# Tuned attention + gMLP kernel: PSUM banks handed out by longest free, products in single banks, and scores placed directly behind a product

## The chip, the cores and the metric

The kernel runs on one core of one Trainium2 chip. The metric is device time in microseconds, median of three runs. All engines of the core take part: TensorE (PE, with its weight loads PEld), VectorE (DVE), ScalarE (ACT), GpSimd (POOL), and SyncE (SP), which issues the transfers.

## The reference

Batch is 8, heads 8, sequence 576, head dimension 64; d_model is 512 and d_ff 1024.

```python
scores = scale * q @ k.T                      # per batch and head
scores = where(block_i >= block_j, scores, -1e9)   # blocks of 64
attn = exp(scores - max); attn = attn / (sum(attn) + 1e-9)
x = (attn @ v) laid out as (B, S, 512)
h = relu(x @ w_in); u, v = h[..., :512], h[..., 512:]
v_n = (v - mean) / sqrt(var + 1e-6)
v_s = einsum('ts,bsd->btd', w_spatial, v_n) + b_spatial
out = (u * v_s) @ w_out
```

## The kernel before

Work is cut by batch, and in a batch by pairs of heads: four pairs per batch, 32 pairs, named b_p (7_3 is the last) and numbered g = 4b + p. Batch 0 has its own opening; batch 1 ("plain") uses the raw q and k; from batch 2 on q and k are split in a high and a low part (`hi`, `lo`).

A pair goes through these steps. SP loads `raw`; ACT, DVE and POOL make `hi` and `lo`. TensorE makes the scores in four parts (lane "S"): parts 0 and 1 in a PSUM tile of two banks each (a double), part 2 in two single banks, part 3 (`scores_last`, called L below, line L568) in a double again. DVE's `rows` (L614, L620) read the scores out of PSUM with the mask and the row maximum; ACT takes exp; POOL and ACT scale; DVE transposes in blocks of 32 (L683); sixteen transfers on SP's queue (L691) regroup the blocks from `p` to `pt`, of which there is one buffer. Then TensorE makes the product (lane "A", tile `av`, L709): a low part of 4 matmuls for the first 256 rows and a high part of 18 for the other 320. Both lie in one double. ACT copies each half out and DVE subtracts (L746), which gives `x`.

The gMLP of a batch (lane "M") is 360 matmuls: `mv` (v half, L1062), `mu` (u half, L1172), `ms` (spatial product, L1209 to L1216), `mo` (output, L1261). Each group of them fills one single bank, which ACT or DVE empties. The first v group of a batch needs all four products of that batch.

PSUM's eight banks are two doubles (`ps_s`, ring `r_s`) and four singles (`ps_m`, ring `r_m`). A ring hands its buffers out in turn: the next taker gets the buffer that was given out longest ago, whether another one is free or not.

Nothing is in the order in which the functions add it. All steps are given to `Line`, which plays them against costs written in the kernel (ns per step, `TURN` for a change of kind on TensorE, `REACH` for a signal) and so fixes each engine's instruction order; on the chip every engine follows its order and waits on semaphores. On TensorE `pick_pe` takes the head of a lane: S and A wait until their inputs have been ready for `SLACK` ns, and the first part of a pair's scores has a gate: not before the M matmuls done (`spent`) amount to (g - LEAD)/4 of a batch's gMLP. In what follows one unit is such a quarter. Where the plan leaves TensorE idle for long, `bridge` fills the gap with pad matmuls (as many as fit in the gap less 300 ns, and none for fewer than three).

Of the kernel before, what the change touches and what calls it, by code (L numbers as in the profile page):

```python
# [17 lines left out]
P = 128  # L18
# [17 lines left out]
LEAD = 5.0  # L36
# [3 lines left out]
    ("A", "S"): 200, ("A", "M"): 250, ("A", "T"): 203, ("M", "A"): 96, ("T", "A"): 96,  # L40
}
REACH = {"PE": 170, "DVE": 125, "ACT": 145, "POOL": 70}
SLACK = {"A": 3500, "S": 1200, "T": 0, "M": 100}


class Ring:
# [5 lines left out]
    def free_at(self, ahead=0):  # L52
        k = len(self.given) + ahead - self.bufs
        if k < 0:
            return 0.0
        if k >= len(self.given) or self.given[k].users:
            return None
        return self.given[k].freed

# [17 lines left out]
class Line:  # L77
# [48 lines left out]
    def pick_pe(self):  # L126
# [12 lines left out]
        late = [k for k in at if not (k == "S" and heads[k].gate is not None and self.spent < heads[k].gate and "M" in at)]  # L139
# [5 lines left out]
    def bridge(self, until):  # L145
# [8 lines left out]
        self.spare.given.append(hold)  # L154
        self.pad("M" if self.kind == "T" else self.kind, n)

    def pick(self, eng):
        if eng == "PE":
            return self.pick_pe()
# [27 lines left out]
    def play(self):  # L187
        while True:
            picks = [(p[0], e, p[1]) for e in self.ENGINES for p in [self.pick(e)] if p]
            if not picks:  # L190
                break
# [3 lines left out]
            for h in op.takes:  # L195
                h.ring.given.append(h)
# [5 lines left out]
            if eng == "PE":  # L202
# [3 lines left out]
                self.kind, self.run = kind, op.first and op.lane  # L206
# [23 lines left out]
def kernel(  # L230
# [32 lines left out]
    ps_s = ctx.enter_context(tc.tile_pool(name="ps_s", bufs=2, space=PSUM))  # L263
    ps_m = ctx.enter_context(tc.tile_pool(name="ps_m", bufs=4, space=PSUM))
# [11 lines left out]
    warm = ps_m.tile([P, 512], F32, tag="m", name="warm")  # L276
# [24 lines left out]
    r_m, r_s = Ring(4), Ring(2)  # L301
# [3 lines left out]
    def pad(kind, n):  # L305
        x = ps_m.tile([P, 512], F32, tag="m", name=f"pad_{next(pads)}")
# [12 lines left out]
    def given(ring, users):  # L319
        h = Hold(ring, users)  # L320
        ring.given.append(h)
        return h

    given(r_m, 0)
# [138 lines left out]
    u_tile = {}  # L463
# [4 lines left out]
    def banks(k, nm):  # L468

        if k == 2:  # L470
            return [ps_m.tile([P, 512], F32, tag="m", name=f"s_{nm}_2_{hd}") for hd in range(2)]
        x = ps_s.tile([P, 2, 512], F32, tag="s", name=f"s_{nm}_{k}")
# [7 lines left out]
    def attention(b, pr):  # L480
# [61 lines left out]
        def scores(k):  # L542
            bk = box["s", k] = banks(k, nm)
# [14 lines left out]
        def scores_last():  # L558
            bk = ps_s.tile([P, 2, 512], F32, tag="s", name=f"s_{nm}_3")
# [15 lines left out]
        for k in range(4):  # L575
# [123 lines left out]
        def start_product():  # L699
            box["av"] = ps_s.tile([P, 2, 512], F32, tag="s", name=f"av_{nm}")  # L700

# [3 lines left out]
        def products(z, todo):  # L705
            for n, (c, q0, q1, move) in enumerate(todo):
                for j in range(2):
                    js = slice(64 * j, 64 * j + 64)
                    nc.tensor.matmul(  # L709
                        box["av"][js, z, q0:q1], box["v"][:, c, js], move(j), start=(n == 0),  # L710
# [3 lines left out]
        def low_product():  # L714
            start_product()
# [14 lines left out]

        a_hold = Hold(r_s, 4)
        al = line.add("PE", 646, low_product, after=[*moved, got_v], takes=[a_hold], lane="A")
        al.first = True
        al.slack = 500 if plain else None
        ah = line.add("PE", 2082, high_product, behind=[al], lane="A", drops=[pt_hold, v_hold])
        ev = []
        for z, (q0, n, src) in enumerate(((0, 256, al), (256, 320, ah))):
            def high(z=z, q0=q0, n=n):
# [4 lines left out]
                nc.scalar.copy(box["x"][:, 0, q0:q0 + n], box["av"][:, z, :n])  # L743

            def low(z=z, q0=q0, n=n):
                nc.vector.tensor_tensor(  # L746
                    out=box["x"][:, 1, q0:q0 + n], in0=box["av"][:, z, :n],
# [6 lines left out]
            h = add("ACT", (269, 321)[z], high, after=[src], takes=takes, drops=[a_hold], rank=0,  # L754
                    behind=ev[:1])
            ev.append(add("DVE", (335, 402)[z], low, after=[h], drops=[a_hold], rank=0))
# [10 lines left out]
    def opening():  # L767
# [65 lines left out]
        def unit(k, pr):  # L833
# [8 lines left out]
            def scores():  # L842
# [7 lines left out]
                if k == 3:  # L850
                    box["s"] = bk = ps_s.tile([P, 2, 512], F32, tag="s", name=f"s_{nm}")
# [5 lines left out]
                box["s"] = bk = banks(k, nm)  # L857
# [77 lines left out]
            for z, (t0, m) in enumerate(split):  # L935
                t_hold = Hold(r_m, 1)

                def transposes(z=z, t0=t0, m=m):
                    box["t", z] = ps_m.tile([P, 512], F32, tag="m", name=f"t_{nm}_{z}")
# [24 lines left out]
            def product():  # L964
                box["av"] = ps_s.tile([P, 2, 512], F32, tag="s", name=f"av_{nm}")
# [63 lines left out]
    def moe(b, ready):  # L1029
# [14 lines left out]
        def v_group(c):  # L1044
# [5 lines left out]
            def bank():  # L1050
                if "ps" not in box:
                    box["ps"] = ps_m.tile([P, 512], F32, tag="m", name=f"mv_{b}_{c}")
                return box["ps"]

# [5 lines left out]
            def mm(n, j, k, w):  # L1060
                a = tails[b][:, k].rearrange("p j t -> p (j t)") if j == 2 else xts[b, k][:, j, cs]
                nc.tensor.matmul(bank(), a, w[:, k, DH:], start=(n == 0), stop=(n == len(todo) - 1))  # L1062
# [99 lines left out]
        def u_group(z, dc):  # L1162
# [6 lines left out]
            def mm(n, j, k, w):  # L1169
                if n == 0:  # L1170
                    box["ps"] = ps_m.tile([P, 512], F32, tag="m", name=f"mu_{b}_{z}_{dc}")
# [25 lines left out]
        def sp_group(z, dc):  # L1197
# [8 lines left out]
            def mm(n, k, a, w):  # L1206
                if n == 0:
                    box["ps"] = ps_m.tile([P, 512], F32, tag="m", name=f"ms_{b}_{z}_{dc}")
# [165 lines left out]
```

## Time and profile before

| | us |
|---|---|
| median of 3 runs | 691.52 (691.37 to 692.26) |
| the profiled execution | 691.11 |
| its span, first to last instruction | 689.3 |
| TensorE busy in it | 664.6 (96%) |
| DVE busy | 495.6 (72%) |
| ACT busy | 369.5 (54%) |
| POOL busy | 344.9 (50%) |

The span is the time between the first and the last instruction; 1.8 us of the execution lie around it. Ends of matmuls are modelled and overlap, so below the distance from one start to the next is used for what a matmul costs.

### The profile page before, as it was taken

Reading aid. Unit: us, or ns where it says so; the run is one execution under the profiler, and the core shown is the slowest. Engines: PE = TensorE matmul, PEld = TensorE weight load, DVE = VectorE, ACT = ScalarE, POOL = GpSimd, SP = SyncE. Lnnn points to the kernel's source line nnn. Section 1 sums busy time; section 2 is a strip of 40 time slices with the busy share of each in tenths; the row PEclk is TensorE's granted clock in tenths of the full one; section 3 lists DMA queues with packets and bytes.
Section 4 is the critical chain, followed back from the end, with each engine's and each line's share of the span. In section 5 each row is a group of like instructions: output and inputs, shape, how many; then the busy total and the mean of one; then the engine's idle time right before and its main releaser. Section 6 shows DMA issues by size and latency. Waiting matters only on the chain.

```text
span 689.3 us, 15505 instructions
## 1 busy us (share of the span) xinstructions
PE 664.6 (96%) x5394; PEld 582.2 (84%) x5394; DVE 495.6 (72%) x1404; ACT 369.5 (54%) x1036; POOL 344.9 (50%) x689
## 2 busy tenths in 40 slices
PE   8999889999999999999999999999999999999998
PEld 5586767888889888988889888898889888898897
DVE  6989789767885778767787678857787677842532
ACT  7879757644654565455655546544654546511320
POOL 4377644545665445664555456644456645520111
PEclk9999999999999999999999999999999999999999
DMA  8164566566456664566555654566645555441002
GB/s 282 48 214 145 143 175 189 152 167 164 126 140 169 159 167 115 130 164 169 142 135 136 162 149 128 135 169 154 159 124 139 152 159 152 98 110 56 1 1 70
DMA packets 44210, 95.57 MB, mean 139 GB/s; under 512 B 9698, under 2 KB 19938, under 8 KB 44132
## 3 DMA queue, kind: packets, MB, share of 16 engines
q1 hardware_dynamic: 44132, 94.58, 50.9%
q8 instruction: 43, 0.70, 0.5%
q14 instruction: 35, 0.29, 0.1%
HBM read 39.23 MB, written 9.44 MB: 71 GB/s over the span
## 4 chain that ended last, share of the span: by engine, by line
PE 32%; DMA 17%; SPq 15%; DVE 14%; ACT 11%; POOL 6%; issue 5%; DVEq 0%; ACTq 0%; POOLq 0%
SPq L691 15%; DMA raw<-qk 11%; PE ms L1209 7%; PE mo L1261 7%; DMA pt<-p 5%; DVE p L683 4%; PE av L709 4%; POOL p L337 4%; DVE p L614 4%; PE mv L1062 3%; ACT hi L516 3%; PE mu L1172 3%; ACT p L642 2%; DVE x L746 2%; PE t L949 2%
## 5 line engine op out<-in xcount | busy, mean ns | idle before, releaser
L642 ACT ACTIVATE p<-p,nmax 128x128 f32<-128x128 f32 (+4 forms) x252 | 145.9, 581 | 50.3 <-DVE nmax L614 39.6
L337 POOL TENSOR_SCALAR p<-p,ssum 128x384 f32<-128x384 f32 (+5 forms) x262 | 151.9, 593 | 20.9 <-DVE ssum L661 6.7
L683 DVE STREAM_TRANSPOSE p<-p 128x384 f32<-128x384 f32 (+2 forms) x196 | 122.2, 641 | 28.5 <-POOL p L337 26.7
L1172 PE MATMUL mu<-x,wi_hi 128*128 128x288 f32 x512 | 110.3, 299 | 1.8 <-ACT vr L1074 1.8
L614 DVE CUSTOM_DVE_ANT_1 p<-s,mask 128x128 f32<-128x128 f32 (+1 forms) x224 | 95.0, 486 | 3.1 <-PE s L552 2.4
L655 POOL TENSOR_SCALAR ssum<-ssum 128x4 f32<-128x4 f32 (+1 forms) x112 | 26.6, 237 | 125.9 <-ACT p L642 111.4
L709 PE MATMUL av<-pt,v 128*64 128x64 f32 (+2 forms) x1232 | 83.0, 290 | 6.4 <-DMA pt<-p 4.8
L709 PEld LDWEIGHTS av<-pt,v 128*64 128x64 f32 x1232 | 65.3, 137 | 27.7 <-issue 10.4
L1172 PEld LDWEIGHTS mu<-x,wi_hi 128*128 128x128 f32 x512 | 85.3, 190 | 3.5 <-ACT vr L1074 2.0
L1062 PE MATMUL mv<-wi_hi,x 128*128 128x512 f32 x256 | 87.4, 400 | 0.0
L1261 PE MATMUL mo<-gh,wo_hi 128*128 128x288 f32 x256 | 76.5, 299 | 0.2
L1209 PE MATMUL ms<-ws_lo,vh 128*128 128x288 f32 x256 | 76.6, 299 | 0.0
L1209 PE MATMUL ms<-ws_hi,vh 128*128 128x288 f32 x256 | 76.5, 299 | 0.0
L1261 PE MATMUL mo<-gh,wo_lo 128*128 128x288 f32 x256 | 76.1, 297 | 0.0
L1261 PE MATMUL mo<-gl,wo_hi 128*128 128x288 f32 x256 | 76.0, 297 | 0.0
L1209 PE MATMUL ms<-ws_hi,vl 128*128 128x288 f32 x256 | 75.7, 296 | 0.0
L1172 PE MATMUL mu<-x,wi_lo 128*128 128x288 f32 x256 | 70.8, 298 | 1.2 <-POOL wi_lo L361 1.2
L516 ACT CAST hi<-raw 128x640 fp32r<-128x640 f32 x48 | 33.3, 726 | 60.2 <-DMA raw<-qk 56.8
L522 POOL TENSOR_TENSOR lo<-raw,hi 128x320 fp32r<-128x320 f32 (+1 forms) x72 | 53.8, 763 | 19.9 <-ACT hi L516 19.9
L1231 ACT CAST gh<-u 128x288 fp32r<-128x288 f32 x64 | 26.4, 429 | 62.7 <-DVE u L1223 45.0
L1062 PEld LDWEIGHTS mv<-wi_hi,x 128*128 128x128 f32 x256 | 48.1, 188 | 12.4 <-issue 2.9
L1234 POOL TENSOR_TENSOR gl<-u,gh 128x288 fp32r<-128x288 f32 x48 | 38.2, 810 | 28.9 <-ACT gh L1231 28.4
(130 smaller groups left out, 1502.9 us busy)
## 6 DMA issues: line engine op xcount, KB each, us to landing
pt<-p SPq DMA_DIRECT2D x448, 100.0 KB, 2.2
raw<-qk SPq DMA_DIRECT2D x28, 640.0 KB, 4.5
v<-v SPq DMA_DIRECT2D x32, 320.0 KB, 3.1
outT<-o SPq DMA_DIRECT2D x64, 144.0 KB, 2.0
rwi<-w_in SPq DMA_DIRECT2D x8, 512.0 KB, 4.3
rwo<-w_out SPq DMA_DIRECT2D x4, 512.0 KB, 4.0
raw<-qk SPq DMA_DIRECT2D x8, 192.0 KB, 4.6
rws<-w_spT SPq DMA_DIRECT2D x4, 288.0 KB, 2.8
```

The source lines that it names most:

```text
L337: nc.gpsimd.tensor_scalar(out=x, in0=x, scalar1=by, scalar2=1.0, op0=ALU.mult, op1=ALU.mult)
L516: nc.scalar.copy(box["hi"][:, cs], box["raw"][:, cs])
L522: eng.tensor_tensor(out=box["lo"][:, cs], in0=box["raw"][:, cs], in1=box["hi"][:, cs].bitcast(F32), op=ALU.subtract,)
L614: nc.vector.tensor_tensor_reduce(out=out, in0=by_block(bk[hd][:, o:o + n]), in1=tiles(mask, 5 - t, t + 1), scale=-0.125, scalar=BIG, op0=A ...
L642: nc.scalar.activation(out, out, AF.Exp, bias=mx, scale=-1.0, accum_out=box["sum", k][:, c:c + 1],)
L683: nc.vector.transpose(x, x)
L691: nc.sync.dma_start(box["pt"][32 * j:32 * j + 32, i], box["pp"][32 * i:32 * i + 32, j])
L709: nc.tensor.matmul(box["av"][js, z, q0:q1], box["v"][:, c, js], move(j), start=(n == 0), stop=(n == len(todo) - 1), skip_group_check=True,)
L1062: nc.tensor.matmul(bank(), a, w[:, k, DH:], start=(n == 0), stop=(n == len(todo) - 1))
L1172: nc.tensor.matmul(box["ps"][:, :HT], w[:, k, ds], xts[b, k][:, j, zs], start=(n == 0), stop=(n == len(todo) - 1),)
L1209: nc.tensor.matmul(box["ps"][:, :HT], vn[k][a][:, ds], w[:, k, zs], start=(n == 0), stop=False)
L1261: nc.tensor.matmul(box[ec, "ps"][:, :HT], w[:, k, es], a[:, k, :], start=(k == 0 and n == 0), stop=(last and n == 2),)
```

## The change

Seven edits, of which the first four belong together.

- Banks are handed out by a new ring, `Banks`: a taker gets the one that has been free longest, and each bank has a tag of its own, so that no taker waits for a certain bank in turn.
- The product's two halves take one single bank each (`a_holds`, in `r_m`) and no double.
- From pair 2_2 on (`MATE + 2`), the first scores of pair g have no gate of their own: they stand directly behind the product of pair g-2 (`first`, `trail`), and that product waits until the `hi` and `lo` of pair g are there. The product has the gate instead, at (g + 2 - 5.5)/4 of a batch for its own g. `op.first` now names the lane that must follow, so parts 0, 1 and 2 of the scores and the product before them stay together; `pick_pe` gets a first try (`hold`) in which such a run is not broken up.
- For the pairs before, `LEAD` is 6 units in place of 5.
- `SLACK` of a product is 2500 in place of 3500 ns (100 in place of 500 in batch 1), and `TURN` from A to S 110 in place of 200.
- In a batch's gMLP seven `ms` groups, not six, stand ahead of the first four `mo` groups; in batch 0 the fifth v group comes one place sooner.
- Making `w_out`'s halves has a lower rank (2.6 in place of 2.1).

```diff
-LEAD = 5.0
+LEAD = 6.0
+MATE, MATE_LEAD = 8, 5.5
...
-SLACK = {"A": 3500, "S": 1200, "T": 0, "M": 100}
+SLACK = {"A": 2500, "S": 1200, "T": 0, "M": 100}
...
+class Banks(Ring):
+    def __init__(self, bufs):
+        self.last = [None] * bufs
+    def free(self):
+        return sorted((h.freed if h else 0.0, n) for n, h in enumerate(self.last) if not h or not h.users)
+    def free_at(self, ahead=0):
+        free = self.free()
+        return free[ahead][0] if ahead < len(free) else None
+    def take(self, hold):
+        hold.at = self.free()[0][1]
+        self.last[hold.at] = hold
...
+        if hold and self.run and self.run == self.kind and self.run in heads and not heads[self.run].left:
+            return None
...
-            if k == "S" and op.gate is not None and self.spent < op.gate and "M" in heads:
+            if k in "SA" and op.gate is not None and self.spent < op.gate and "M" in heads:
...
+    def bank(hold, name):
+        return ps_m.tile([P, 512], F32, tag=f"m{hold.at}", name=name)
+
+    def double(hold, name):
+        return ps_s.tile([P, 2, 512], F32, tag=f"s{hold.at}", name=name)
...
-            op.first = k < 2
+            op.first = "S" if k < 2 else None
             op.waive = k == 3
             if k == 0:
-                op.gate = (g - LEAD) * MOE_NS / NPAIR
+                if g < MATE + 2:
+                    op.gate = (g - LEAD) * MOE_NS / NPAIR
+                else:
+                    first, last = mates[g - 2]
+                    last.trail.append(op)
+                    op.left += 1
+                    for d in need:
+                        d.trail.append(first)
+                    first.left += len(need)
...
-        a_hold = Hold(r_s, 4)
-        al = line.add("PE", 646, low_product, after=[*moved, got_v], takes=[a_hold], lane="A")
-        al.first = True
-        al.slack = 500 if plain else None
-        ah = line.add("PE", 2082, high_product, behind=[al], lane="A", drops=[pt_hold, v_hold])
+        a_holds = [Hold(r_m, 2), Hold(r_m, 2)]
+        al = line.add("PE", 646, low_product, after=[*moved, got_v], takes=a_holds[:1], lane="A")
+        al.first = "A"
+        if g >= MATE:
+            al.gate = (g + 2 - MATE_LEAD) * MOE_NS / NPAIR
+        al.slack = 100 if plain else None
+        ah = line.add("PE", 2082, high_product, behind=[al], takes=a_holds[1:], lane="A", drops=[pt_hold, v_hold])
+        ah.first = "S" if MATE <= g < B * NPAIR - 2 else None
+        mates[g] = al, ah
...
-        order = "vuvuvuvuvuuuu" if b else "vvvvuuuuuuvuu"
+        order = "vuvuvuvuvuuuu" if b else "vvvvuuuuuvuuu"
...
-        return front[:1], front[1:] + sp[:ND + 2] + out[:NO] + sp[ND + 2:], out[NO:]
+        return front[:1], front[1:] + sp[:ND + 3] + out[:NO] + sp[ND + 3:], out[NO:]
...
-    ready["o"] = [x for c in range(ND) for x in prep_w_out(c, 2.1)]
+    ready["o"] = [x for c in range(ND) for x in prep_w_out(c, 2.6)]
```

What the plan makes of it is seen in the order of instructions. First TensorE at the scores of pair 7_3. In the names `s_7_3_0` is part 0 of the scores, `s_7_3_3` the last part L, `mu_6_1_3` an M group of batch 6, `av_7_1` the product of pair 7_1; the last number of a name only tells buffers apart. Before:

```order
L1172 MATMUL mu_6_1_3_8019<-x_6_2_7137,wi_hi_114 128x288
L1172 MATMUL mu_6_1_3_8019<-x_6_3_7409,wi_hi_114 128x288
L552 MATMUL s_7_3_0_8039<-hi_7_3_7904 128x128 x2
L552 MATMUL s_7_3_0_8039<-lo_7_3_7905,hi_7_3_7904 128x128 x2
L552 MATMUL s_7_3_0_8039<-hi_7_3_7904,lo_7_3_7905 128x128 x2
```

and now:

```order
L750 MATMUL av_7_1_1_8010<-pt_7_1_7762,v_7_1_7660 64x64 x2
L750 MATMUL av_7_1_1_8010<-pt_7_1_7762,v_7_1_7660 64x128 x2
L750 MATMUL av_7_1_1_8010<-pt_7_1_7762,v_7_1_7660 64x64 x4
L587 MATMUL s_7_3_0_8038<-hi_7_3_7876 128x128 x2
L587 MATMUL s_7_3_0_8038<-lo_7_3_7877,hi_7_3_7876 128x128 x2
L587 MATMUL s_7_3_0_8038<-hi_7_3_7876,lo_7_3_7877 128x128 x2
```

The scores moved from behind an M group to behind a product; this is so at 22 pairs (2_2 to 7_3), and at pair 1_3. Between the first three parts and L stand 9 M matmuls for pair 7_3 now, and 12 before.

Next DVE ahead of the rows of the same pair. `vr`, `st`, `vl` and `vs_a` belong to the normalization of v groups 3 and 4 of batch 6, `x_7_1` is the product's subtraction. Before:

```order
L1122 TENSOR_SCALAR vr_6_3_7872<-vr_6_3_7872,st_6_3_7873 128x512
L1187 TENSOR_SCALAR u_6_7632<-mu_6_1_2_7995 128x288
L1154 TENSOR_TENSOR vl_6_3_8013<-vr_6_3_7872,vh_6_3_8012 128x512
L1122 TENSOR_SCALAR vr_6_4_7918<-vr_6_4_7918,st_6_4_7919 64x512
L1187 TENSOR_SCALAR u_6_7632<-mu_6_1_3_8019 128x288
L1138 TENSOR_TENSOR vs_a_122<-vr_6_4_7918,vs_b_123 64x512
L614 ISA p_7_3_8074,nmax_7_3_0_8075<-s_7_3_0_8039,mask_93 128x4x32
```

and now:

```order
L1163 TENSOR_SCALAR vr_6_3_7940<-vr_6_3_7940,st_6_3_7941 128x512
L1123 TENSOR_TENSOR vr_6_4_7998<-mv_6_4_7957,vr_6_4_7998 64x512
L1127 TENSOR_SCALAR vr_6_4_7998<-vr_6_4_7998 64x512
L790 TENSOR_TENSOR x_7_1_8032<-av_7_1_0_8003,x_7_1_8032 128x256
L1135 BN_STATS st_6_4_7999<-vr_6_4_7998 64x6
L1136 BN_AGGR st_6_4_7999<-st_6_4_7999 64x2
L1195 TENSOR_TENSOR vl_6_3_8030<-vr_6_3_7940,vh_6_3_8029 128x512
L790 TENSOR_TENSOR x_7_1_8032<-av_7_1_1_8010,x_7_1_8032 128x320
L657 ISA p_7_3_8067,nmax_7_3_0_8068<-s_7_3_0_8038,mask_93 128x4x32
```

The rows moved ahead of the last two steps of v group 4, and behind the product's two subtractions.

Last, the pads on TensorE, of which before there were 3, 8, 8 and 14, and now 3, 17, 13, 3, 11 and 4. The first 3 are in the opening; the 17 stand ahead of the first `mu` group, the 13 ahead of the first `ms` group, the 3 ahead of the product 2_1, the 11 ahead of the product 2_3, the 4 ahead of the last product, 7_3. The row of the last ones before:

```order
L1209 MATMUL ms_6_1_3_8375<-ws_hi_118,vl_6_3_8013 128x288
L1214 MATMUL ms_6_1_3_8375<-ws_a_120,vs_a_122 128x288
L1216 MATMUL ms_6_1_3_8375<-ws_b_121,vs_b_123 128x288
L314 MATMUL pad_3_8396<-ident_92 128x128 x14
L709 MATMUL av_7_3_8411<-pt_7_3_8243,v_7_3_7955 64x256 x2
```

and now:

```order
L1250 MATMUL ms_6_1_3_8424<-ws_hi_118,vl_6_3_8030 128x288
L1255 MATMUL ms_6_1_3_8424<-ws_a_120,vs_a_122 128x288
L1257 MATMUL ms_6_1_3_8424<-ws_b_121,vs_b_123 128x288
L350 MATMUL pad_5_8453<-ident_92 128x128 x4
L750 MATMUL av_7_3_0_8458<-pt_7_3_8300,v_7_3_8204 64x256 x2
```

The place is the same, ten pads fewer. Between the scores L of pair 7_3 and the product 7_2 stand 82 M matmuls now and 45 before; between the products 7_2 and 7_3 stand 102 (103 before). On SP's queue two stores stand between the sixteen transfers of `pt_7_3` now, four before.

More of the change, by code (lines that the diff above doesn't have):

```diff
@@ L153, in bridge, with pick @@
         hold.freed = now + n * PAD_NS
-        self.spare.given.append(hold)
-        self.pad("M" if self.kind == "T" else self.kind, n)
-    def pick(self, eng):
+        self.spare.take(hold)
+        self.pad("M" if self.kind == "T" else self.kind, n, hold)
+    def pick(self, eng, hold):
         if eng == "PE":
-            return self.pick_pe()
+            return self.pick_pe(hold)
         now, best = self.free[eng], None
@@ L188, in play @@
         while True:
[L189 to L190 removed]
+            for hold in (True, False):
+                picks = [(p[0], e, p[1]) for e in self.ENGINES for p in [self.pick(e, hold)] if p]
+                if picks:
+                    break
+            else:
                 break
@@ L205, in play @@
                 end = start + TURN.get((self.kind, kind), 0) + ns
-                self.kind, self.run = kind, op.first and op.lane
+                self.kind, self.run = kind, op.first
                 if kind == "M" and op.lane == "M":
@@ L300, with pad @@
     add = line.add
-    r_m, r_s = Ring(4), Ring(2)
     r_raw, r_hi, r_lo, r_v, r_pp, r_pt, r_x, r_xs = (Ring(n) for n in (1, 1, 1, 2, 2, 1, 6, 2))
     r_u, r_gh, r_gl, r_vr, r_o, r_vn, r_vs = (Ring(n) for n in (1, 1, 1, 2, 2, 1, 1))
-    def pad(kind, n):
-        x = ps_m.tile([P, 512], F32, tag="m", name=f"pad_{next(pads)}")
+    def pad(kind, n, hold):
+        x = bank(hold, f"pad_{next(pads)}")
         for k in range(n):
@@ L459, in prep_w_tail, with banks @@
         return [a, b, c, d, e]
-    u_tile = {}
+    mates = {}
     def by_block(x):
         return x.rearrange("p (j x) -> p j x", j=4)
-    def banks(k, nm):
+    def banks(k, nm, holds):
         if k == 2:
-            return [ps_m.tile([P, 512], F32, tag="m", name=f"s_{nm}_2_{hd}") for hd in range(2)]
-        x = ps_s.tile([P, 2, 512], F32, tag="s", name=f"s_{nm}_{k}")
+            return [bank(holds[hd], f"s_{nm}_2_{hd}") for hd in range(2)]
+        x = double(holds[0], f"s_{nm}_{k}")
         return x[:, 0], x[:, 1]
@@ L558, in scores_last @@
         def scores_last():
-            bk = ps_s.tile([P, 2, 512], F32, tag="s", name=f"s_{nm}_3")
+            bk = double(s_hold[3][0], f"s_{nm}_3")
             box["s", 3] = bk
@@ L753, in attention @@
                 takes = [x_hold[b, pr]] + ([xs_hold[b]] if pr == 0 else [])
-            h = add("ACT", (269, 321)[z], high, after=[src], takes=takes, drops=[a_hold], rank=0,
+            h = add("ACT", (269, 321)[z], high, after=[src], takes=takes, drops=[a_holds[z]], rank=0,
                     behind=ev[:1])
-            ev.append(add("DVE", (335, 402)[z], low, after=[h], drops=[a_hold], rank=0))
+            ev.append(add("DVE", (335, 402)[z], low, after=[h], drops=[a_holds[z]], rank=0))
         x_done[b, pr] = ev
@@ L850, in scores @@
                 if k == 3:
-                    box["s"] = bk = ps_s.tile([P, 2, 512], F32, tag="s", name=f"s_{nm}")
+                    box["s"] = bk = double(s_hold[0], f"s_{nm}")
                     for z in range(2):
@@ L964, in product @@
             def product():
-                box["av"] = ps_s.tile([P, 2, 512], F32, tag="s", name=f"av_{nm}")
+                box["av"] = double(a_hold, f"av_{nm}")
                 vt, pt = boxes[pr]["v"], box["pt"]
```

55 lines of the change are left out of this document (28 added, 27 removed).

## The prediction

> **What bounds the kernel now.** I read the page first, for the share of each engine.
>
> ```profile
> PE   664.6 (96%) x5394; PEld 582.2 (84%) x5394; DVE 495.6 (72%) x1404; ACT 369.5 (54%) x1036; POOL 344.9 (50%) x689
> PEclk9999999999999999999999999999999999999999
> ```
>
> TensorE is busy nearly throughout at full clock, and its real work is the same before and after. So the time can change in three ways only: what a change of kind costs on TensorE, how long it waits, and how many pads it runs. The view of waits by engine comes second.
>
> ```profile
> PE s L568 <- DVE nmax L614: 5.7, 7, 1.5
> PE av L709 <- DMA pt<-p: 4.8, 4, 2.6
> PE s L552 <- DVE x L746: 2.2, 2, 1.5
> PE mu L1172 <- ACT vr L1074: 1.8, 1, 1.8
> PE av L709 <- issue: 1.3, 2, 1.1
> PE mu L1172 <- POOL wi_lo L361: 1.2, 1, 1.2
> ```
>
> The columns are total us, times, longest. The waits of the first row are L waiting for the rows of its pair to leave the double; they lie at pairs 2_3 to 7_3 nearly alone, all over the run. The others but a few tenths are in the early stage (batch 1) and at the last product. Third comes TensorE's timeline, for what a change of kind costs.
>
> ```profile
> 299.10 0.29 PE L1209 MATMUL ms<-ws_hi,vh 128*128 128x288 f32 x1
> 299.33 2.96 PE L709 MATMUL av<-pt,v 128*64 128x256 f32 x44
> 302.22 0.40 PE L1209 MATMUL ms<-ws_lo,vh 128*128 128x288 f32 x1
> 302.46 0.29 PE L1209 MATMUL ms<-ws_hi,vl 128*128 128x288 f32 x1
> 302.60 0.29 PE L1214 MATMUL ms<-ws_a,vs_a 128*128 128x288 f32 x1
> ...
> 88.87 2.96 PE L709 MATMUL av<-pt,v 128*64 128x256 f32 x44 [2.65 <-DMA pt<-p]
> 91.76 0.93 PE L552 MATMUL s<-raw 64*128 64x128 f32 x8
> ...
> 589.47 0.30 PE L1172 MATMUL mu<-x,wi_lo 128*128 128x288 f32 x1
> 589.60 0.69 PE L1172 MATMUL mu<-x,wi_hi 128*128 128x288 f32 x4
> 590.22 0.33 PE L552 MATMUL s<-hi 64*128 64x128 f32 x2
> ```
>
> M matmuls of 288 columns start 0.13 apart (302.46 to 302.60). After a product the second M starts 0.24 behind the first (302.22 to 302.46): the restart costs 0.11. Into the scores, four M from 589.60 would end a step at 590.13, and the scores start at 590.22: 0.09. From the start of a product to the next start it is 2.89 whether M follows (299.33 to 302.22) or scores do (88.87 to 91.76, the one place before where they do).
>
> **The joins.** Before, a pair costs M to product, product to M, M to scores, scores to M. Now the middle two become one, product to scores. By the rows that step costs what product to M did (2.89 both), so what goes is 0.09 and the restart of 0.11: 0.20 a pair. The row of 88.87 is of batch 1, whose scores are not split; for the split ones there is no row, and the bounds are 0 (the join costs both steps that it replaces) and 0.30 (it costs nothing, and 0.10 more goes, which is what 299.10 to 299.33 has over a step). I take 0.20, the nearest row. For the 19 joins from pair 3_1 on that is 3.8 us (0 to 5.7); three more, and 1_3, lie in the early stage.
>
> By the Trainium skill, TensorEngine Tiling (Array Packing), Key Properties, a change of tiling mode drains TensorE, and a product (128 rows by 64 columns) and scores (64 by 128) are different modes, so that the join is no seamless step. The trace agrees as far as it goes: 88.87 to 91.76 is no shorter than 299.33 to 302.22. Without that rule and that row one would put the upper bound, 5.7 in place of 3.8.
>
> **The early stage** (69.8 to 223.7, the end of product 2_3). The rows of its pads and of the step of its products:
>
> ```profile
> 69.82 1.95 PE L314 MATMUL pad<-ident 128*128 128x128 f32 x16
> 139.29 2.96 PE L709 MATMUL av<-pt,v 128*64 128x256 f32 x44 [1.55 <-DMA pt<-p]
> 220.24 2.97 PE L709 MATMUL av<-pt,v 128*64 128x256 f32 x44
> 223.14 0.40 PE L1209 MATMUL ms<-ws_lo,vh 128*128 128x288 f32 x1
> 618.67 3.29 PE L314 MATMUL pad<-ident 128*128 128x128 f32 x28
> 623.08 2.97 PE L709 MATMUL av<-pt,v 128*64 128x256 f32 x44 [1.12 <-issue]
> ```
>
> A pad is two records; 28 take 3.29 less some 0.15 of overlap, 0.224 a pad. Before there are 16 pads here, 3.6, and waits of 10.5: all of the third, fourth and sixth rows of the waits (5.2), 4.5 of the transfers', 0.2 of issue, 0.6 of L. Together 14.1. Now 44 pads stand here, 9.9. What waits stay? The scores no longer wait for a product to leave a double (2.2), since products have left the doubles. The 3.0 of `mu` are about what the nine added pads ahead of `mu` cover. The transfers' 4.5 stay: the products of batch 1 are one `pt` buffer and sixteen transfers apart, and neither changes. And each of four pad groups leaves the 0.3 to 0.5 that `bridge` doesn't fill, 1.6. So 9.9 + 4.5 + 1.6, less four joins 0.8, is 15.2: 1.1 us more than before. Bounds: no waits but the 1.6, a gain of 3.4; all of the 10.5 stay, a loss of 5.5. The new LEAD, the fifth v group's place and the later `w_out` act only in this stage, through the pads that are counted; no `mo` waits for `w_out` in the view. M done early is not worth anything by itself here: the first v group of batch 2 needs product 2_3, and the eleven pads stand just ahead of it.
>
> **L and the new neighbours on DVE**, from pair 3_1 on. What L needs is the fourth row of its pair.
>
> ```profile
> 531.04 0.33 PE L552 MATMUL s<-hi 64*128 64x128 f32 x2
> 534.33 0.31 PE L568 MATMUL s<-hi 128*128 128x320 f32 x1
> ...
> 593.89 0.29 PE L1209 MATMUL ms<-ws_hi,vl 128*128 128x288 f32 x1
> 595.00 0.41 PE L568 MATMUL s<-hi 128*128 128x320 f32 x1 [0.82 <-DVE nmax L614]
> ```
>
> ```profile
> 532.04 0.29 DVE L614 CUSTOM_DVE_ANT_1 p<-s,mask 128x128 f32<-128x128 f32 x1 [0.44 <-PE s L552]
> ...
> 532.81 0.42 DVE L614 CUSTOM_DVE_ANT_1 p<-s,mask 128x256 f32<-128x256 f32 x1
> ...
> 593.03 0.69 DVE L1138 TENSOR_TENSOR vs_a<-vr,vs_b 64x512 fp32r<-64x512 f32 x1 [0.32 <-ACT vs_b L1134]
> 593.75 0.29 DVE L614 CUSTOM_DVE_ANT_1 p<-s,mask 128x128 f32<-128x128 f32 x1
> ...
> 594.52 0.42 DVE L614 CUSTOM_DVE_ANT_1 p<-s,mask 128x256 f32<-128x256 f32 x1
> ...
> 606.48 0.83 DVE L683 STREAM_TRANSPOSE p<-p 128x640 f32<-128x640 f32 x1
> 607.24 0.45 DVE L746 TENSOR_TENSOR x<-av,x 128x320 fp32r<-128x320 f32 x1
> ```
>
> At pair 6_1 the rows begin 1.00 after the scores, the fourth is through at 533.23 (532.81 + 0.42), and L comes at 534.33, 3.29 after the scores, with 1.1 to spare. At 7_3 they begin 3.53 after the scores (590.22 to 593.75), behind `vs_a`: 2.5 late, of which the order allowed for 0.5 (12 M, not 8), and L starts 0.06 after the fourth row. It is DVE's lateness that L pays, not the number of banks. Now at the x_3 pairs (3_3 to 7_3) the order allows only 0.1 (9 M), which costs 0.4; of the work ahead of the rows `vs_a` goes (0.7), and the product's second subtraction comes (0.45). These about cancel, so I keep 0.8 at five pairs, 4.0. At the other joins the subtraction takes 0.45 of the 1.1: hidden while DVE is on time; I put 0.5 for all 17. So 4.5, against 5.4 before (5.1 of L, 0.3 of the transfers): -0.9. Bounds: 0, all waits gone, 5.4 better; and 15 (five at 1.5, the longest of the view, and 17 at 0.45), 10 worse. The new takers of single banks, the product's halves and part 2 of the scores right behind, cost nothing as long as the first subtraction is through in the 3.4 from the end of the low half to part 2 (2.2 of the product and 1.2 of parts 0 and 1); with DVE 2.5 late that cover still holds.
>
> The product now waits for the next scores' `hi` and `lo`. Scores never waited for these before: the view of waits has no such row, so 0. Of seven `ms` groups ahead of `mo`, only the last batch can feel the order: there POOL's three `gl` steps, 0.81 each, must pass between the fourth `mo` group and the fifth; one `ms` group (14 of 0.13) and the first nine `mo` matmuls (1.2) hide these 2.4: 0, at most 0.5.
>
> ```profile
> L1234 POOL TENSOR_TENSOR gl<-u,gh 128x288 fp32r<-128x288 f32 x48 | 38.2, 810 | 28.9 <-ACT gh L1231 28.4
> ```
>
> **The end.** Product 7_2 ended and M went on at 604.90; 103 M and 14 pads later product 7_3 started at 623.08: 18.2.
>
> ```profile
> 604.90 0.40 PE L1209 MATMUL ms<-ws_lo,vh 128*128 128x288 f32 x1
> ...
> 607.38 7.07 SPq L691 DMA_DIRECT2D pt<-p  x9
> 615.13 1.14 SPq L691 DMA_DIRECT2D pt<-p  x2
> pt<-p SPq DMA_DIRECT2D x448, 100.0 KB, 2.2
> ```
>
> The transfers began at 607.38, when the last transpose was through (606.48 + 0.83), 12.3 after L at 595.00. Now 82 M (0.13 each, 11.0) and the product (2.9) lie between L and the end of product 7_2, so the transposes are through ahead of that end. Sixteen issues of 0.6 (the row of two, with its spacing), two stores of 0.7 (607.38 + 7.07 to 615.13) and 2.2 to land make 13.3. TensorE has 102 M (13.6), 4 pads (0.9) and the rest that the bridge leaves (0.4): 14.9, which is longer and hides it. 18.2 to 14.9 is a gain of 3.3. Bounds: 4.6 (if even the pads' time were not needed) and 1.2 (a long issue as in the row of nine, 7.07 for what should be 5.7, and a store waiting).
>
> **Sum**, on the profiled execution's 691.1 (a span of 689.3 and 1.8 around it; the median is 0.4 above): 691.1 - 3.8 (joins) + 1.1 (early) - 0.9 (L and DVE) - 3.3 (end) = 684.2.
>
> **Rivals.**
> - The waits of L go altogether. They are the same gap at the same place in each batch, and the 4.5 would not come: 679.7. For it: products leave the doubles. Against: the row of `vs_a` ahead of the rows. By the Trainium skill, Perfetto Trace Analysis, Optimization Strategy, consistent bubbles can mean that there isn't enough PSUM for the next tile; by that rule this is the likelier case, but the trace shows the double held by a late reader. 0.14.
> - The early stage keeps all its waits and pays the pads on top (loss of 5.5, not 1.1): 688.6. For it: nothing is sooner in batch 1's transfers. 0.08.
> - On the other side: DVE. Behind each join two subtractions and ten row steps crowd into 4 us, and DVE falls behind at every join as it does at 7_3 now. From 0.4 more a join (22 joins) the change loses over 0.2%; at 0.5, 11 us, it is 695. For it: the 1.1 to spare less 0.45 is 0.65, and DVE was 2.5 late at 7_3. Against: L waited 7 times in all before. 0.09.
> - Joins save nothing (the lower bound) and the early stage loses 3 more: 691.0, no difference. 0.07.
>
> **Chances.** My forecast, 681 to 688, has 0.62. Faster or slower by 0.2% (1.4 us) is about what can be told from no change. Faster: 0.62 + 0.14 + 0.08, less a little for the tails, 0.82; no difference 0.09; slower 0.09. The range from 679.5 to 690 takes in the first two rivals and leaves out the last two.
>
> **What would show it.** Right: at pairs from 3_1 on a product's start and that of the scores 2.9 apart; no wait of scores for `x`; product 7_3 some 15 after the end of 7_2; L still waiting about 1 us at x_3 pairs; product 2_3 at about 222. Wrong: L or part 2 of the scores waiting at most joins; product 2_3 past 226; a distance well over 2.9.

## The result, and the profile after

The changed kernel takes 673.54 us (median of 6 runs, 671.56 to 675.63) against 691.44 for the kernel before in the same sessions: a ratio of 0.9746 (95% interval 0.9724 to 0.9768). It is 17.9 us faster where 6.9 were forecast (691.1 to 684.2). The profiled execution took 671.56, 2.0 below that median; its span is 669.8, 19.5 below the span of before (689.3). The sums below go from span to span. The granted clock was 1.000 in this execution and 0.995 to 0.999 in the five others; what that means for the early stage stands in the part on the prediction.

From the page, the shares and TensorE's clock:

```profile
PE   656.6 (98%) x5430; PEld 583.2 (87%) x5430; DVE 492.6 (74%) x1382; ACT 376.2 (56%) x1059; POOL 353.2 (53%) x688
PEclk9999999999999999999999999999999999999999
```

The view of waits by engine (total us, times, longest), the four largest rows of TensorE:

```profile
PE av L750 <- DMA pt<-p: 3.9, 3, 1.7
PE av L750 <- DVE u L1228: 2.7, 2, 2.6
PE warm L316 <- DVE mask L298: 1.1, 1, 1.1
PE s L907 <- DMA raw<-qk: 0.8, 1, 0.8
```

L is L603 now. It has no row, and neither have the scores waiting for `x` or `mu` waiting for weights. What is left from batch 1 on is products waiting. TensorE's timeline at pair 7_3 (start, us, then the instruction), the place where L waited 0.8 before:

```profile
567.86 3.07 PE L750 MATMUL av<-pt,v 128*64 128x256 f32 x44
570.86 0.33 PE L587 MATMUL s<-hi 64*128 64x128 f32 x2
...
572.98 0.40 PE L1213 MATMUL mu<-x,wi_lo 128*128 128x288 f32 x1
573.22 0.30 PE L1213 MATMUL mu<-x,wi_hi 128*128 128x288 f32 x1
...
574.29 0.31 PE L603 MATMUL s<-hi 128*128 128x320 f32 x1
575.11 0.29 PE L1213 MATMUL mu<-x,wi_hi 128*128 128x288 f32 x1
```

and DVE's at the same place:

```profile
571.25 0.65 DVE L1195 TENSOR_TENSOR vl<-vr,vh 128x512 fp32r<-128x512 f32 x1
571.83 0.48 DVE L790 TENSOR_TENSOR x<-av,x 128x320 fp32r<-128x320 f32 x1
572.23 0.27 DVE L657 CUSTOM_DVE_ANT_1 p<-s,mask 128x128 f32<-128x128 f32 x1
...
572.99 0.41 DVE L657 CUSTOM_DVE_ANT_1 p<-s,mask 128x256 f32<-128x256 f32 x1
```

The rows begin 1.37 after the scores (572.23 less 570.86), where it was 3.53 before. The fourth is through at 573.40, and L starts 0.89 later: it waits for nothing. From pair 3_1 on the rows begin 1.00 to 1.38 after the scores at every pair, and L has 0.87 to 1.23 to spare; before, the first figure went up to 4.22 and the second down to 0.06. One joined pair ahead of that stretch is an exception: at 2_3 the scores stand behind a product too, and the rows still begin 2.78 after them, behind `vs_a` and the second subtraction. There 11 M stand ahead of L, and L loses only 0.1.

```profile
184.98 0.33 PE L587 MATMUL s<-hi 64*128 64x128 f32 x2
```

```profile
186.64 0.69 DVE L1179 TENSOR_TENSOR vs_a<-vr,vs_b 64x512 fp32r<-64x512 f32 x1 [0.35 <-ACT vs_b L1175]
187.35 0.49 DVE L790 TENSOR_TENSOR x<-av,x 128x320 fp32r<-128x320 f32 x1
187.76 0.28 DVE L657 CUSTOM_DVE_ANT_1 p<-s,mask 128x128 f32<-128x128 f32 x1
```

The whole span, taken apart by what follows what on TensorE, is the table below. Each step is the distance from one start to the next; an M step counts 0.132 (`mu`, `ms`, `mo`) or 0.231 (`mv`), 424.4 in all in every kernel, and what it takes over that goes into a row. The third column is the first experiment. Transposes, products themselves and the rest agree within 1 us.

| us (steps) | before | changed | no joins |
|---|---|---|---|
| first M after a product, over its step | 2.95 (28) | 0.63 (6) | 3.00 (28) |
| last M ahead of scores, over its step | 2.57 (28) | 0.36 (4) | 2.40 (26) |
| M waiting ahead of L | 6.99 (8) | 0 | 0 |
| scores and L, with the waits ahead and inside | 105.7 | 100.5 | 103.3 |
| late steps inside `mu` | 5.03 (18) | 0.08 (1) | 3.76 (9) |
| late steps inside `mo` | 2.73 (21) | 0.39 (3) | 1.33 (6) |
| waits ahead of products | 5.60 (7) | 6.79 (4) | 9.70 (7) |
| pads (records) | 8.82 (66) | 12.10 (102) | 8.87 (76) |
| sum | 140.4 | 120.9 | 132.4 |

The sum falls by 19.5, as the span does. The joins (first two rows) are 4.5 of that, 0.10 and 0.09 each. The waits of L are 7.0; the view lists 5.7, since it counts from the modelled end of the M ahead. "Products themselves" hides two shifts: the opening's products take 0.7 less, and five joined products take 0.8 more, because a step inside them comes late.

### The profile page after: what moved, and what is told of

Read it like the earlier page. It is cut to its first block, busy times and chain, and to the rows that moved or that the text cites. A ratio compares the mean times of both kernels' runs of the same rounds, so it can differ in the third digit from the quotient of the medians.

```text
span 669.8 us, 15587 instructions
## 1 busy us (share of the span) xinstructions
PE 656.6 (98%) x5430; PEld 583.2 (87%) x5430; DVE 492.6 (74%) x1382; ACT 376.2 (56%) x1059; POOL 353.2 (53%) x688
## 4 chain that ended last, share of the span: by engine, by line
PE 87%; SPq 5%; ACT 3%; DVE 2%; DMA 2%; issue 1%; POOL 1%; POOLq 0%; ACTq 0%
PE mo L1302 14%; PE mv L1103 14%; PE ms L1250 14%; PE mu L1213 12%; PE av L750 12%; PE s L587 8%; SPq L734 5%; PE s L603 3%; PE t L993 2%; PE av L1021 2%; ACT p L951 1%; PE ms L1255 1%; PE pad L350 1%; PE ms L1257 1%; PE s L907 1%
## 5 line engine op out<-in xcount | busy, mean ns | idle before, releaser
L372 POOL TENSOR_SCALAR p<-p,ssum 128x128 f32<-128x128 f32 (+5 forms) x261 | 152.2, 596 | 20.4 <-DVE ssum L704 8.8
L750 PEld LDWEIGHTS av<-pt,v 128*64 128x64 f32 x1232 | 63.9, 137 | 28.5 <-issue 5.8
L790 DVE TENSOR_TENSOR x<-av,x 128x256 fp32r<-128x256 f32 (+1 forms) x56 | 25.4, 454 | 50.6 <-ACT x L787 50.2
L787 ACT CAST x<-av 128x256 fp32r<-128x256 f32 (+1 forms) x56 | 22.4, 399 | 69.2 <-PE av L750 69.1
L557 POOL TENSOR_TENSOR lo<-raw,hi 128x320 fp32r<-128x320 f32 (+1 forms) x72 | 57.7, 815 | 2.7 <-ACT hi L551 2.4
```

The lines of the kernel that those rows point to most:

```text
L372: nc.gpsimd.tensor_scalar(out=x, in0=x, scalar1=by, scalar2=1.0, op0=ALU.mult, op1=ALU.mult)
L557: eng.tensor_tensor(out=box["lo"][:, cs], in0=box["raw"][:, cs], in1=box["hi"][:, cs].bitcast(F32), op=ALU.subtract,)
L750: nc.tensor.matmul(box["av", z][js, q0:q1], box["v"][:, c, js], move(j), start=(n == 0), stop=(n == len(todo) - 1), skip_group_check=True,)
```

## The experiments

**No joins.** All other edits stay.

```diff
-MATE, MATE_LEAD = 8, 5.5
+MATE, MATE_LEAD = 99, 5.5
```

> The changed kernel without the joins: single banks for the product, banks by longest free and all other edits stay, but scores stand behind M matmuls as before. Theory (a product of 2.9 us ahead of the scores gives DVE that long without new work from TensorE, so that the rows start on time): L waits again, 4 to 6 us in all, and the 0.19 a pair of the joins (3.7) goes; about 682 to 683. Rival (L waited because the product held a double): no wait of L comes back, only the 3.7 are lost; about 677.

681.97 us (ratio to before 0.9876, 0.9832 to 0.992). The time is what the theory said, the reason is not: no wait of L came back (third column). The rows begin 1.8 to 2.1 after the scores at two of four pairs of a batch, but 11 or 15 M stand ahead of L there. So joins aren't needed to keep L from waiting. Without them the first two rows of the table give 4.4 back, and the rest comes from waits of products, of scores for `lo` (1.9 in the view), of `mu` and of `mo`, less fewer pads.

**Banks and singles alone, banks alone, LEAD alone, no joins with LEAD 5.** These say which edit takes L's waits away. The first is the kernel before with edits one and two; the second has the product in a double as well (the line that matters; the matmuls then write the two halves of that double):

```diff
-        a_holds = [Hold(r_m, 2), Hold(r_m, 2)]
+        a_holds = [Hold(r_s, 4)] * 2
```

the third is the kernel before with LEAD changed, and the fourth is the kernel without joins with it changed back:

```diff
-LEAD = 5.0
+LEAD = 6.0
```

```diff
-LEAD = 6.0
-MATE, MATE_LEAD = 8, 5.5
+LEAD = 5.0
+MATE, MATE_LEAD = 99, 5.5
```

> The kernel before with the first two edits alone: banks by longest free, the product in single banks; gates, LEAD, SLACK, TURN and the orders as before. Theory F (L waited because the product held a double, so that scores came in turn with it): no wait of L, none of scores for x, the 2.3 of the mo groups gone; about 681. Theory P (L waited because the rows came late behind the normalization, and LEAD sets where the scores fall against that): L waits 4 us or more; about 687 to 689.

> The kernel before with the first edit alone: doubles and singles handed out by longest free, the product still in a double. Theory F: a double is still held by the product, L waits 4 us or more; 688 to 691, less 2.3 if the steps of the mo groups go with the rings. Rival (the ring alone, since L may then take whichever double is free): no wait of L; 682 to 684.

> The kernel before with LEAD 6 in place of 5 and nothing else. Theory F: L waits as before, 5 us or more; 689 to 692. Theory P: the scores of the x_3 pairs fall elsewhere against the normalization of the v groups, L waits under 2 us; 684 to 687.

> The kernel without joins (682.0), now with LEAD 5 in place of 6. Theory F: no wait of L; 681 to 683. Theory P: L waits 4 us or more at x_3 pairs; 686 to 688.

Measured: 687.83 (0.9961, 0.9942 to 0.998); 690.01 (0.9989, 0.9968 to 1.001, no difference); 704.15 (1.0184, 1.0162 to 1.0206); 689.47 (0.9978, 0.996 to 0.9996). One row each of their waits, in this order; in the last kernel L waits nowhere, and products wait 16.1 in all:

```profile
PE s L603 <- DVE nmax L657: 4.0, 5, 1.4
```

```profile
PE s L603 <- DVE nmax L657: 5.7, 7, 1.7
```

```profile
PE s L552 <- DVE x L746: 10.8, 9, 3.7
```

```profile
PE av L750 <- DMA pt<-p: 5.7, 5, 2.3
```

Theory F falls: with the product out of the doubles L still waits 4.0, at the same pairs, because the rows there begin 3.0 to 4.1 after the scores, as before. Nor does longest free help by itself. LEAD 6 alone does take L's waits away (0.3 left), but scores then wait 10.8 for the double in which a product lies, and one `ms` waits 4.8 for `vs_a`. So L's waits go with the place of the scores, which the joins, LEAD, or (last kernel) the other small edits each shift. Theory P was right on L's waits with LEAD 6 (its time, 684 to 687, was 17 us too low) and wrong on those of the last kernel, where theory F was right on the waits and 6 us too low on the time. The single banks are what lets scores move ahead without waiting for `x`.

**The changed kernel with one of the first two edits undone.** Banks in turn (`Banks` gives the one given out longest ago; below the change in `take`, `free_at` follows it), and the product in a double (the second diff above).

```diff
     def take(self, hold):
-        hold.at = self.free()[0][1]
+        hold.at = self.n % len(self.last)
+        self.n += 1
         self.last[hold.at] = hold
```

> The changed kernel with banks handed out in turn again; joins and single banks for the product stay. Theory (the joins do it): L waits at no more than a few pairs; 673 to 676, with a difference only in the early stage, where pads fall away. Rival (longest free is what spares L its waits): 5 us or more of waits of L; 679 or more.

> The changed kernel with the product in a double again; joins and longest free stay. By the profile of the changed kernel the second subtraction at pair 7_3's join ends 1.5 after the first scores start, and part 1 of the scores would start 0.7 after them: if part 1 needs the product's double, it waits some 0.8 at each of 22 joins; 690. Rival (the single banks only matter without joins): 674.

773.5 us (1.1198, 1.1142 to 1.1253) and 725.34 (1.0505, 1.0459 to 1.0552). The largest rows of their waits:

```profile
PE mo L1302 <- DVE u L1264: 21.1, 6, 4.5
```

```profile
PE s L587 <- DVE x L792: 36.5, 24, 2.7
```

Both expectations were wrong by their size. Joined scores with the product in a double wait for its second subtraction at each of the joins, 1.5 each and not 0.8 (2.34 at 7_3): part 1 needs the double, and the second subtraction there ends 3.15 after the scores have started (623.78 against 620.63), behind three steps of the normalization. The first row of the pair begins 3.07 after the scores there (623.70), again with a product directly ahead. In turn, M groups wait for a bank behind its reader, and the granted clock of that run is 0.952. Without joins the first edit brings nothing clear of noise (0.1%) and both together 0.4%; with joins, taking either one away makes the kernel 5 to 12% slower than before.

**Joins half a unit sooner.**

```diff
-MATE, MATE_LEAD = 8, 5.5
+MATE, MATE_LEAD = 8, 6.0
```

> The changed kernel with the products' gate half a unit sooner (MATE_LEAD 6.0), so that product and joined scores fall elsewhere against the normalization of the v groups. Theory J (the 2.9 us of product ahead of the scores are what puts the rows on time, wherever the join falls): the rows start 1.0 to 1.4 after the scores at all pairs, no wait of L; 672 to 676. Theory P (the place of the scores against the normalization decides, and 5.5 happens to be a good one): at one of the four pairs of a batch the rows start over 2.2 late and L waits 3 us or more in all; 676 to 680.

673.89 us (0.975, 0.9728 to 0.9772), the same as the changed kernel. TensorE and DVE at pair 7_3, where now `mv` and not `mu` stands around the join:

```profile
565.16 2.96 PE L750 MATMUL av<-pt,v 128*64 128x256 f32 x44
568.06 0.33 PE L587 MATMUL s<-hi 64*128 64x128 f32 x2
```

```profile
569.08 0.29 DVE L657 CUSTOM_DVE_ANT_1 p<-s,mask 128x128 f32<-128x128 f32 x1
```

The rows begin 1.02 after the scores here, 1.00 to 1.02 at all pairs from 5_0 on, and at most 1.78 at the pairs between 3_1 and 4_3. From 3_1 on no pair has L waiting. Theory J holds at this second place from 3_1 on, but for 1.78 at one pair. It is no general rule: at the joined pair 2_3 the rows begin 2.72 after the scores here too, and with the product in a double 3.07 after them at pair 7_3. At these two places of the join the rows come in time for L; the join isn't the only way to that, and it isn't a guarantee.

**More work on DVE.** Three statistics of the mask ahead of each pair's first row, from pair 3_0 on, unknown to the plan.

```diff
+                    if i == 0 and r == 0 and g >= MATE + 4:
+                        for z in range(3):
+                            junk = st_p.tile([P, 8], F32, tag="junk", name=f"junk_{nm}_{z}", bufs=1)
+                            nc.vector.bn_stats(out=junk[:, 0:6], in_=mask.rearrange("p a t k -> p (a t k)")[:, :512])
```

> The changed kernel with three bn_stats of the mask on DVE (0.70 each, results unused) ahead of the first row of each pair from 3_0 on, 2.1 us a pair that the plan doesn't know of. By the trace of the changed kernel L starts 0.87 to 1.24 after its fourth row has ended. If that spare is all there is, L waits 0.9 to 1.2 at each of the 20 pairs, some 21 us, and the kernel takes about 694; each later step of DVE that something waits for would add to that. If DVE catches the time up ahead of the rows (it is busy 74% of the span): under 680.

703.0 us (1.0165, 1.0137 to 1.0193). DVE's added work ahead of one pair's rows, and L's row of the waits:

```profile
602.93 2.13 DVE L650 BATCH_NORM_STATS2 junk<-mask 128x6 f32<-128x512 f32 x3
```

```profile
PE s L603 <- DVE nmax L661: 16.5, 20, 1.3
```

By the distances M waits 19.7 ahead of L in 20 pairs, 0.99 each: 2.13 less the spare of 0.87 to 1.23. The spans differ by 32.7 (702.5 and 669.8). The other 13 us are late steps inside products (6.0), `ms` waiting for `vs_a` (3.6), scores and L (3.1) and waits ahead of products (1.2), less 0.7 of pads. So DVE has about 1 us to spare at a join, and no more.

**Seven `ms` groups or six.**

```diff
-        return front[:1], front[1:] + sp[:ND + 3] + out[:NO] + sp[ND + 3:], out[NO:]
+        return front[:1], front[1:] + sp[:ND + 2] + out[:NO] + sp[ND + 2:], out[NO:]
```

> The changed kernel with six ms groups ahead of the first mo groups, as before, in place of seven. Theory (the seventh group is what took the steps of 0.23 to 0.44 out of the mo groups): 2.4 us come back there and one at the last product (9 pads in place of 4); about 677. Rival (those steps went with the banks): about 674 to 675.

675.92 us (0.9789, 0.9747 to 0.9832). The late steps of `mo` stay at 0.7; they were not the seventh group's. They are 4.5 with banks alone, 0.4 with LEAD 6 alone and 1.3 without joins, so that they go with the order as a whole; which edit moves them is open.

**Fewer joins.** From pair 3_2 and from 3_0 on, without the early pads that these leave out: `MATE` 12 and 10.

```diff
-MATE, MATE_LEAD = 8, 5.5
+MATE, MATE_LEAD = 12, 5.5
```

> The changed kernel with joins from pair 3_2 on in place of 2_2 (MATE 12): four joins fewer, and the 3 and the 11 pads of batch 1's end fall out of the order. If pads stand only where TensorE would have been idle anyway and the gap is set by product 2_3's inputs: 673 to 675 (four joins at 0.20 lost, the rest the same). If the early joins made those gaps, by holding M back behind the gate of the product: 14 pads of 0.224 (3.1) come off against 0.8; about 671. A wait of L for its rows at batch 2's pairs without a join would cost 1 to 2 more.

> The changed kernel with joins from pair 3_0 on (MATE 10): two joins fewer, the 3 pads ahead of product 2_1 gone, 12 in place of 11 ahead of 2_3. Between the kernel changed and the one with joins from pair 3_2 on: 672 to 674.

674.03 (0.9749, 0.9722 to 0.9776) and 673.96 us (0.9745, 0.9726 to 0.9765): no difference from the changed kernel. Four joins less and 14 pads less cancel with waits of products (8.5 against 6.8) and of scores for `lo` (1.2).

**The pads of the early stage.** The changed kernel without the 17 and 13 (numbers 1 and 2 of its pads), and, in the same function, the kernel before with `n = 17` for its pad number 1, ahead of `mu`:

```diff
-        x = bank(hold, f"pad_{next(pads)}")
+        nth = next(pads)
+        if nth in (1, 2):
+            return
+        x = bank(hold, f"pad_{nth}")
```

> The changed kernel without the 17 pads ahead of the first mu group and the 13 ahead of the first ms group (6.7 us of pads), same order otherwise. Theory W (the pads stand where TensorE would wait for the weights, and keep its clock up): waits of mu and ms of 5 to 7 us take their place, and the clock halves for some 3 us as in the kernel before; 673 to 676. Rival (the pads delay M that was ready): 668 to 671.

> The kernel before with 17 pads ahead of its first mu group in place of 8, nothing else. Theory W: the two waits of mu (1.2 and 1.8) shrink by the 2.0 of the added pads, and the 1.7 that the halved clock cost goes; 688.5 to 690. Rival (the clock drop has nothing to do with the wait): the granted clock still is about 0.5 for 3.4 us, and the time stays at 691 to 692.

671.24 us (0.9725, 0.9709 to 0.9741) and 694.58 (1.0056, 1.0036 to 1.0076). The granted clock (the column ahead of the last two, DMA share and GB/s) over stretches of the kernel before, of the changed kernel without the early pads, and of the kernel before with 17 pads:

```profile
80.30:83.70 3.40, 3.40 (x17) 3.40 (x16) 1.82 (x6) 2.13 (x8) 1.42 (x1) 0.51 0.59 158
```

```profile
74.00:77.00 3.00, 3.00 (x15) 3.00 (x14) 3.00 (x7) 1.17 (x2) 2.08 (x2) 0.50 0.79 234
```

```profile
89.00:94.00 5.00, 4.63 (x35) 3.38 (x37) 0.34 (x1) 0.00 (x0) 0.00 (x0) 0.51 0.51 198
```

Without the pads the waits come back as theory W said (0.9 and 2.4 of `mu`, 1.2 of `ms`), and the half clock behind them. But the first product, 1_0, starts at 88.56 instead of 88.09, and the last of the stage, 2_3, at 217.84 instead of 218.29. With the 17 pads in the kernel before, `mu` waits 1.1 in place of 3.0 at full clock, and then the first product waits longer, 5.0 in place of 2.65, and starts at 89.36 in place of 88.87; the half clock follows that wait:

```profile
89.36 5.14 PE L712 MATMUL av<-pt,v 128*64 128x256 f32 x44 [4.97 <-DMA pt<-p]
```

In all four kernels product 1_0 starts between 88.1 and 89.4, though TensorE's work ahead of it ends between 84.4 and 87.5. What sets it are its transfers. In the changed kernel the row names a `u` of DVE, which ended at 87.94, but the last transfer landed at 87.89, 0.05 sooner. SP's last issues of them, in the kernel before and in the changed one (start, us they take, queue):

```profile
80.05 7.11 SPq L691 DMA_DIRECT2D pt<-p  x10
```

```profile
82.94 3.38 SPq L734 DMA_DIRECT2D pt<-p  x5
```

They end at 87.16 and 86.32, and product 1_0 starts 1.7 and 1.8 later. Pads and waits ahead of it are paid out of the same gap. My expectation for the second kernel, 688.5 to 690, missed that.

**Side by side, without pads.** One session, five rounds, the changed kernel again, without the early pads, and without any but the opening's three (`if nth in (1, 2, 3, 4, 5)`).

> The changed kernel once more, as the measure for the two beside it: 673 to 674.

> The changed kernel without the 17 and 13 pads, beside the changed kernel in one session. If the pads only replace waits, the two agree within 1 us; if the 671.2 measured before is a gain: 2 us or more below the changed kernel.

> The changed kernel without any pad but the opening's three (48 pads less, 10.8 us of pads). If pads only fill what would be waited for: within 1 us of the changed kernel, plus 1.7 for each stretch of half clock that comes with a wait. If pads delay work: up to 3 us faster.

674.83 us (0.9746, 0.972 to 0.9773), 672.88 (0.9735, 0.9706 to 0.9764) and 671.52 (0.9714, 0.9689 to 0.9739). The last median is 3.3 below the first, but the intervals overlap: the pads gain nothing, and whether they cost 2 to 3 us isn't settled. At the end they do cost: without the four ahead of product 7_3, the product starts 13.7 after the end of 7_2 and doesn't wait. By its ratio to the kernel before this is the fastest kernel of the study; the first run without early pads has the lowest median (671.24), in another session, and the intervals overlap.

## Why the prediction was wrong

The direction was right, the time below the range. Term by term:

**The joins: right.** Forecast 0.20 a pair, 3.8 for the 19 from 3_1 on. Measured 0.10 for the restart and 0.09 into the scores, 3.7 for the same stretch (1.9 and 1.8). A start of a product to the start of its scores is 2.89 to 2.90 but at the x_3 pairs, where it is 3.0 to 3.1 (567.86 to 570.86; 3.27 once) because a step inside the product comes late. Products had no such steps before; they take back 0.8, which the 3.7 doesn't count.

**L and DVE: the step that failed.** Forecast 0.9 better, measured 7.1 for the same stretch: 6.2 of waits ahead of L, all there were, and 0.9 of waits ahead of products. Of the 6.2 between the two, 4.5 are waits that I kept and that didn't come; 1.7 are the view's 5.4 for what is 7.1 from start to start. The step was "These about cancel, so I keep 0.8 at five pairs": I counted which DVE steps moved ahead of the rows and which behind, 0.45 against 0.7, and took DVE's lateness of 2.5 as given. What the runs showed in its place: DVE reaches the rows 1.00 to 1.38 after the scores at all pairs of the stretch, and L waits nowhere. Before, at 7_3, DVE was not only behind but idle itself, 0.81 in three places between the scores and the rows (0.32 and 0.17 below, 0.32 ahead of `vs_a`); now it goes from 567.01 into the rows without a wait that the view lists.

```profile
590.93 0.71 DVE L1154 TENSOR_TENSOR vl<-vr,vh 128x512 fp32r<-128x512 f32 x1 [0.32 <-ACT vh L1150]
591.81 0.54 DVE L1122 TENSOR_SCALAR vr<-vr,st 64x512 f32<-64x512 f32 x1 [0.17 <-POOL st L1115]
```

Why it is on time is my reading and not shown by itself: I didn't count TensorE's time. Before, M matmuls ran up to the scores, and their groups and the steps of the normalization stood ahead of the rows; now 2.9 us of product run ahead of the scores, in which TensorE asks only two subtractions of DVE. Joins at another place agree with it (but for 1.78 once); pair 2_3 and the product in a double (2.78 and 3.07 behind a product) show that the order of the steps on DVE counts as well. That the joins alone did it isn't shown either, since a shift by LEAD does it too.

The rival "the waits of L go altogether" had the right outcome, with 0.14. Its ground was that products leave the doubles, and that alone doesn't do it: with the product in singles, and neither joins nor the other edits, L waits 4.0. By the Trainium skill, Perfetto Trace Analysis, Optimization Strategy, consistent bubbles can mean too little PSUM for the next tile. For L's wait the runs disagree: two doubles, fully free of products, still had it. It fits better the scores' wait for `x`, which grew to 10.8 where LEAD 6 met the product in a double.

**`mo`: not in the sum.** 2.4 us of late steps in its groups, 0.1 to 0.3 each, are gone. The view of waits lists hardly any of them, so that I didn't see them; distances from start to start do.

**The early stage: wrong by 3.6 in this execution, by 0.4 in another.** Forecast 1.1 longer, measured 2.5 shorter, the opening's end included (product 2_3 starts 1.95 sooner, with four M more done by then). The pads are as counted, 9.8 for the 44, and what the groups leave at their end is 0.2 or less, not 0.3 to 0.5. The products' waits are 6.5, not 4.5. Their rows, with the pads ahead of `mu` and of 2_3:

```profile
68.52 3.96 PE L350 MATMUL pad<-ident 128*128 128x128 f32 x34
...
88.09 1.27 PE L750 MATMUL av<-pt,v 128*64 128x256 f32 x11 [2.58 <-DVE u L1228]
103.85 2.96 PE L750 MATMUL av<-pt,v 128*64 128x256 f32 x44 [1.23 <-DMA pt<-p]
119.82 0.44 PE L750 MATMUL av<-pt,v 128*64 128x256 f32 x2 [0.99 <-DMA pt<-p]
137.22 1.09 PE L750 MATMUL av<-pt,v 128*64 128x256 f32 x10 [1.70 <-DMA pt<-p]
...
215.75 2.62 PE L350 MATMUL pad<-ident 128*128 128x128 f32 x22
218.29 2.96 PE L750 MATMUL av<-pt,v 128*64 128x256 f32 x44
```

What was missing on the side of before was 1.7 us of half clock behind the wait of `mu` (16 steps of 0.24 in place of 0.13) and 1.3 that the opening now ends sooner (pads at 68.52, before 69.82).

The half clock is partly luck of the execution. In the second trace of the changed kernel, with no edit, two products of this stage ran at half clock, and each took 1.7 more than 2.90:

```profile
88.24 4.63 PE L750 MATMUL av<-pt,v 128*64 128x256 f32 x44 [2.35 <-DVE u L1228]
138.83 4.63 PE L750 MATMUL av<-pt,v 128*64 128x256 f32 x44 [2.07 <-DMA pt<-p]
```

There product 2_3 starts at 221.48 and the stage is 0.7 longer than before, counted in the same way. The span, 673.0, is 3.2 above the first trace's, and the two products are 3.3. So this term lies between 2.5 shorter and 0.7 longer, and the 19.5 between the two spans holds more luck than the 17.9 between the medians. The deeper fault is the adding up: product 1_0 starts only 0.8 sooner and 1_1 not at all (88.09 and 103.85, before 88.87 and 103.83), since they wait for transfers, so what TensorE spends ahead of them on pads or waits isn't a cost. The gain comes after 1_1, where scores no longer wait for `x`: 1_2 and 1_3 start 1.9 and 2.1 sooner.

**The end: right.** 18.2 became 14.6 (forecast 14.9), 102 M and four pads without a wait:

```profile
588.99 0.40 PE L1250 MATMUL ms<-ws_hi,vl 128*128 128x288 f32 x1
...
602.62 1.05 PE L350 MATMUL pad<-ident 128*128 128x128 f32 x8
603.60 2.97 PE L750 MATMUL av<-pt,v 128*64 128x256 f32 x44
```

Together: 3.7 + 7.1 + 2.4 + 2.5 + 3.6 is 19.3 of the 19.5; left out are 1.3 less inside scores and L and the 0.8 more inside products, which partly cancel. Three slips of the prediction change none of this by more than 0.1: the pair at 531.04 is 7_0 and not 6_1, product 2_3 ended at 223.2 (220.24 + 2.97) and not at 223.7, and from 3_1 on there are 14 joins beside the x_3 pairs and not 17. Of the rivals, "DVE falls behind at every join" had a sound price: with 2.13 us more DVE work a pair, L paid 0.99 a pair. DVE was on time instead.

## What to carry to other kernels

When an engine is late for a piece of work, look at what its supplier does just ahead, not only at what it has queued itself: a stretch that gives it little to do may let it catch up, if its own order leaves the room. Edits that only free buffers can be worth nothing alone and be what makes a reordering possible, so each should be priced with and without the other. Where one wait sets a point in time, waits and pads ahead of it share one gap and must not be added; and steps from start to start show late steps that a view of waits leaves out. A term of one or two microseconds that comes from the clock should be read in more than one execution.

## What the runs showed of the hardware

A wait of 1.8 us ahead of one M matmul (1.2 more some six us earlier) was followed by 3.4 us at a granted clock of 0.51. So were one of 2.4 with 0.9 just ahead of it, and one of 5.0. One of 2.6 ahead of product 1_0, in the kernel before and in the first trace of the changed one, was not; in the second trace of the changed kernel one of 2.35 at the same place was, and one of 2.07 ahead of 1_3. So the length of a wait doesn't settle it, and what does is open. Each time 1.6 to 2.2 us were lost (16 M at 0.24 in place of 0.13; product 1_0 taking 5.07, with 17 pads, in place of 2.90).

By the Trainium skill, TensorE: Matmul & The Clock Gate, Why this matters for your kernels, gaps of more than about 3 us between bursts of matmuls are to be avoided, since one window of idle brings the clock back to half. The traces show it halved behind shorter waits too, down to 1.8 (with 1.2 ahead of it) and 2.07 (alone).
